# Loading the input in halves, warm-up matmuls and one-bank PSUM tiles in a GEGLU feed-forward kernel

## The chip, the cores and the metric

The kernel runs on one core of one Trainium2 chip. The metric is the device time of one execution in microseconds (us). The text gives the median of all executions of a kernel. A ratio is the mean time of one kernel's fast runs over the mean time of the kernel before's fast runs of the same rounds, so it is not quite the ratio of the medians quoted beside it. A profiled execution has a span 1.8 us shorter than its device time (309.2 against 310.99 us before), so spans are compared with spans.

PE is TensorE's matmul, PEld its weight load, DVE is VectorE, ACT is ScalarE, SPq is the sync engine's queue, which issues all transfers here. A transfer lands when all of its data has arrived. wg, wu and wd are the on-chip copies of w_gate, w_up and w_down.

## The reference

```python
B, S, D, F = 32, 32, 1024, 3584           # all bf16
def reference(x, w_gate, w_up, w_down):
    return (gelu_tanh(x @ w_gate) * (x @ w_up)) @ w_down
```

There are 1024 tokens. x is [1024, 1024] (2.1 MB), and each weight matrix has 3.67 million elements (7.3 MB).

## The kernel before

The kernel works in two phases. Phase one computes gate and up for one block of 128 features ("feature tile", ft, 28 of them) at a time, for all 1024 tokens, and forms gT, the product of the activated gate and up. Phase two multiplies gT by w_down. Weights come in chunks of 1, 3, 4, 4, 4, 4, 4, 4 feature tiles, with two buffers. A PSUM tile of 128x1024 f32 is two banks, and there are four such buffers.

```python
    for c in (1, 3):                       # first chunks; the rest are 4
        ...
    pspool = ctx.enter_context(tc.tile_pool(name="psum", bufs=4, space=PSUM))
    xT = xpool.tile([P, DT, N], bf16, name="xT")
    nc.sync.dma_start_transpose(out=xT[:, :, :], in_=xf)        # all of x at once
    ...
    for ci, FC in enumerate(chunks):
        nc.sync.dma_start(out=wg[:, :, :fw], in_=wg_r[:, :, f0 : f0 + fw])
        nc.sync.dma_start(out=wu[:, :, :fw], in_=wu_r[:, :, f0 : f0 + fw])
        for fl in range(FC):
            gate_ps = pspool.tile([P, N], fp32, name="gate_ps", tag="acc")   # two banks
            up_ps = pspool.tile([P, N], fp32, name="up_ps", tag="acc")
            for wt, ps in ((wg, gate_ps), (wu, up_ps)):
                for nb in range(NNB):              # two halves of 512 tokens
                    for dt in range(DT):           # 8 steps of 128 along D
                        nc.tensor.matmul(ps[:, nsl], lhsT=wt[:, dt, fsl],
                                         rhs=xT[:, dt, nsl], ...)
            # h, sq, w, z, s, hu, gT: three ACT and four DVE operations on [P, 1024]
            ...
        nc.sync.dma_start(out=wd[:, c0 : c0 + FC, :], in_=wd_r[:, c0 : c0 + FC, :])

    for tt in range(NT):
        out_ps = pspool.tile([P, D], fp32, name="out_ps", tag="acc")         # two banks
        for db in range(NDB):
            for ft in range(FT):
                nc.tensor.matmul(out_ps[:, dsl], lhsT=gT[:, ft, tsl], rhs=wd[:, ft, dsl], ...)
            o_sb = opool.tile([P, DB], bf16, name="o_sb", tag="o_sb")
            nc.vector.tensor_copy(o_sb, out_ps[:, dsl])
            nc.sync.dma_start(out=of[tsl, dsl], in_=o_sb)
```

## Time and profile before

| what | before |
|---|---|
| median time (the first 6 of 16 runs) | 310.92 us (310.54 to 312.26) |
| span of the profiled run | 309.2 us |
| PE busy | 291.7 us, 94% |
| first matmul starts | 12.02 us |
| last matmul ends, last copy starts | 305.92 us |

The first lines of the page give the span, and the busy time of each engine with its share of the span.

```profile
span 309.2 us, 3085 instructions
PE 291.7 (94%) x1318; PEld 131.9 (43%) x1344; DVE 95.9 (31%) x128; ACT 86.4 (28%) x86; POOL 0.2 (0%) x4
```

DVE and ACT are busy for a third of the time: PE is the bound. The chain that ended last shows where the rest of the span is. Its columns are start, length (us) and what ran.

```profile
0.73 7.53 SPq L80
8.32 3.65 DMA wg<-in_w_gate_dram
12.02 5.74 PE gate_ps L102 x16
17.75 3.45 PE up_ps L102 x16
...
251.87 10.74 PE out_ps L136 x49
262.66 10.82 PE out_ps L136 x49
...
298.93 0.70 DVE o_sb L144
299.68 6.22 PE out_ps L136 x28
305.92 0.69 DVE o_sb L144
```

Sixteen matmuls take 3.45 us, so one takes 0.216 us, and the 1344 matmuls of the kernel about 290.1 us. The first matmul waits 12.02 us, 7.53 of them for the queue to issue the x transpose. The first sixteen matmuls take 5.74 us, 2.29 more than sixteen later ones. At 298.93 PE waits for a copy of o_sb (0.78 us in the waits of PE). The copy, the store and the end of the kernel take 3.28 us after 305.92. One more detail was in plain sight and was passed over in the prediction: nearly all pieces of 49 matmuls in phase two take 10.82 us, but one takes 10.74.

The timeline of the weight loads shows why the first sixteen are slow. Its columns are start, length, engine, line, operation, count, and in brackets the idle time before it with what ended it.

```profile
12.42 0.15 PEld L102 LDWEIGHTS <-wg 128*128 128x128 bf16 x1 [0.28 <-issue]
...
15.83 0.15 PEld L102 LDWEIGHTS <-wg 128*128 128x128 bf16 x1 [0.28 <-issue]
16.26 1.00 PEld L102 LDWEIGHTS <-wg 128*128 128x128 bf16 x5 [0.28 <-issue]
```

From 12.03 to 16.26 us there are ten steps from one weight load to the next of about 0.427 us (the first is 0.39), twice the later 0.216 us (15.83 to 16.26 is the last such step). The Trainium skill, "TensorE: Matmul & The Clock Gate", Part 1, says that the PE starts at half clock and gets its full clock only after sustained activity of about 3.4 us. The trace agrees in kind: ten matmuls, 4.25 us, at half rate. The granted clock that the profile gives does not show it; it reads 1.00 in each of those microseconds.

### The profile page before, as it was taken

To read this page: it belongs to the slowest core of one execution; us is meant where nothing else is said; L and a number is where in the kernel's file an instruction comes from. 1 tells how busy PE (TensorE), PEld (TensorE's weight loads), DVE (VectorE), ACT (ScalarE), POOL (GpSimd) and SP (SyncE) were. 2 spreads that over 40 slices of the span, in tenths; PEclk is the share of its full clock that TensorE was granted. 3 is DMA by queue.
4 is the path that set the end of the run, shared out by engine and by line. 5 is a ranking of instruction groups with operands and counts; after the bars stand their busy time and mean duration, and the time that the engine had idled before them with its cause. 6 is when DMAs were issued, how large, how long until landed. Compare 5 with 4: busy or idle time off the path is not lost.

```text
span 309.2 us, 3085 instructions
## 1 busy us (share of the span) xinstructions
PE 291.7 (94%) x1318; PEld 131.9 (43%) x1344; DVE 95.9 (31%) x128; ACT 86.4 (28%) x86; POOL 0.2 (0%) x4
## 2 busy tenths in 40 slices
PE   0499999999999999999999999999999999999985
PEld 0144444444444444444444444444444444444442
DVE  0024333444443334444433334442001001100010
ACT  1045344444333444344334443440000000000000
POOL 0000000000000000000000000000000000000000
PEclk9999999999999999999999999999999999999999
DMA  8999994025006101700530000000000100000010
GB/s 197 258 354 371 389 325 144 2 84 188 0 2 209 64 2 27 244 0 2 157 114 2 0 0 0 2 0 17 19 17 17 34 19 17 17 34 19 17 34 17
DMA packets 30892, 26.40 MB, mean 85 GB/s; under 512 B 10912, under 2 KB 27296, under 8 KB 30880
## 3 DMA queue, kind: packets, MB, share of 16 engines
q1 hardware_dynamic: 30880, 26.22, 26.9%
q8 instruction: 10, 0.16, 0.2%
q14 instruction: 2, 0.02, 0.0%
HBM read 22.02 MB, written 2.10 MB: 78 GB/s over the span
## 4 chain that ended last, share of the span: by engine, by line
PE 94%; SPq 2%; DMA 1%; issue 1%; DVE 0%
PE gate_ps L102 32%; PE out_ps L136 31%; PE up_ps L102 31%; SPq L80 2%; DMA wg<-in_w_gate_dram 1%; DVE o_sb L144 0%
## 5 line engine op out<-in xcount | busy, mean ns | idle before, releaser
L102 PE MATMUL gate_ps<-xT,wg 128*128 128x512 bf16 x440 | 102.8, 385 | 12.4 <-DMA wg<-in_w_gate_dram 12.0
L102 PE MATMUL up_ps<-xT,wu 128*128 128x512 bf16 x439 | 100.6, 379 | 0.5
L136 PE MATMUL out_ps<-wd,gT 128*128 128x512 bf16 x439 | 97.1, 379 | 1.3 <-DVE o_sb L144 0.8
L102 PEld LDWEIGHTS <-wg 128*128 128x128 bf16 x448 | 44.3, 99 | 66.2 <-DMA wg<-in_w_gate_dram 12.0
L136 PEld LDWEIGHTS <-gT 128*128 128x128 bf16 x448 | 43.8, 98 | 54.4 <-issue 2.5
L102 PEld LDWEIGHTS <-wu 128*128 128x128 bf16 x448 | 43.8, 98 | 52.9
L111 ACT ACTIVATE h<-gate_ps 128x1024 bf16<-128x1024 f32 x28 | 28.7, 1024 | 84.9 <-PE gate_ps L102 82.3
L115 DVE TENSOR_SCALAR w<-sq 128x1024 bf16<-128x1024 bf16 x28 | 11.9, 426 | 111.7 <-ACT sq L113 111.7
L119 ACT ACTIVATE s<-z 128x1024 bf16<-128x1024 bf16 x28 | 29.6, 1057 | 36.5 <-DVE z L117 36.5
L144 DVE CAST o_sb<-out_ps 128x512 bf16<-128x512 f32 x16 | 11.1, 692 | 85.8 <-PE out_ps L136 85.8
L121 DVE TENSOR_TENSOR hu<-h,up_ps 128x1024 bf16<-128x1024 bf16 x28 | 34.2, 1221 | 8.4 <-PE up_ps L102 8.1
L113 ACT ACTIVATE sq<-gate_ps 128x1024 bf16<-128x1024 f32 x28 | 28.5, 1018 | 0.0
L122 DVE TENSOR_TENSOR gT<-hu,s 128x1024 bf16<-128x1024 bf16 x28 | 19.4, 692 | 3.9 <-ACT s L119 1.1
L117 DVE TENSOR_TENSOR z<-w,h 128x1024 bf16<-128x1024 bf16 x28 | 19.4, 692 | 0.9
L111 ACT ACT_TABLE_LOAD x1 | 1.3, 1283 | 0.7 <-PEq L160 0.7
L119 ACT ACT_TABLE_LOAD x1 | 1.3, 1283 | 0.0
L160 POOL MEMSET const-bfloat16-1.0<- 128x1 bf16 x1 | 0.1, 101 | 0.0
L160 POOL MEMSET const-uint8-127<- 128x1 uint8 x1 | 0.1, 101 | 0.0
L160 POOL MEMSET const-float32-0.0<- 128x1 f32 x1 | 0.1, 98 | 0.2 <-issue 0.2
L160 POOL MEMSET const-float32-1.0<- 128x1 f32 x1 | 0.1, 98 | 0.0
## 6 DMA issues: line engine op xcount, KB each, us to landing
wg<-in_w_gate_dram SPq DMA_DIRECT2D x6, 1024.0 KB, 5.3
wu<-in_w_up_dram SPq DMA_DIRECT2D x6, 1024.0 KB, 5.4
wd<-in_w_down_dram SPq DMA_DIRECT2D x6, 1024.0 KB, 11.9
out_dram<-o_sb SPq DMA_DIRECT2D x16, 128.0 KB, 1.7
wg<-in_w_gate_dram SPq DMA_DIRECT2D x1, 768.0 KB, 6.4
wu<-in_w_up_dram SPq DMA_DIRECT2D x1, 768.0 KB, 8.3
wd<-in_w_down_dram SPq DMA_DIRECT2D x1, 768.0 KB, 9.6
wg<-in_w_gate_dram SPq DMA_DIRECT2D x1, 256.0 KB, 3.7
```

What stands on the lines that cost most here:

```text
L80: nc.sync.dma_start_transpose(out=xT[:, :, :], in_=xf)
L102: nc.tensor.matmul(ps[:, nsl], lhsT=wt[:, dt, fsl], rhs=xT[:, dt, nsl], start=(dt == 0), stop=(dt == DT - 1),)
L111: nc.scalar.activation(h, gate_ps, ACT.Copy)
L113: nc.scalar.activation(sq, gate_ps, ACT.Square)
L115: nc.vector.tensor_scalar(w, sq, _C2A, _C2, ALU.mult, ALU.add)
L117: nc.vector.tensor_tensor(z, w, h, ALU.mult)
L119: nc.scalar.activation(s, z, ACT.Sigmoid)
L121: nc.vector.tensor_tensor(hu, h, up_ps, ALU.mult)
L122: nc.vector.tensor_tensor(gT[:, ft, :], hu, s, ALU.mult)
L136: nc.tensor.matmul(out_ps[:, dsl], lhsT=gT[:, ft, tsl], rhs=wd[:, ft, dsl], start=(ft == 0), stop=(ft == FT - 1),)
L144: nc.vector.tensor_copy(o_sb, out_ps[:, dsl])
L160: nc = _bacc.Bacc("TRN2", target_bir_lowering=False, num_devices=1)
```

## The change

The intent is to start PE earlier and with its clock up. The changed kernel
- transposes x in two halves of 512 tokens, and works through the first four feature tiles for the first half before it needs the second;
- runs 24 matmuls on a tile of zeros while the data arrives;
- uses first chunks of 2 and 2 feature tiles in place of 1 and 3;
- uses PSUM tiles of one bank (128x512) in 8 buffers for gate, up and out, and 3 work buffers in place of 2, so that each ACT and DVE operation of phase one handles half as many columns;
- loads wd in seven pieces of four feature tiles, from the third chunk on, and orders each but the last behind that chunk's weights, without a wait.

```diff
-    for c in (1, 3):
+    for c in (2, 2):
...
-    ework = ctx.enter_context(tc.tile_pool(name="ework", bufs=2))
+    ework = ctx.enter_context(tc.tile_pool(name="ework", bufs=3))
-    pspool = ... name="psum", bufs=4
+    pspool = ... name="psum", bufs=8
+    warm = xpool.tile([P, 512], bf16, name="warm")
+    nc.vector.memset(warm, 0.0)
+    warm_ps = pspool.tile([P, 512], fp32, name="warm_ps", tag="acc")
+    for _ in range(24):
+        nc.tensor.matmul(warm_ps, lhsT=warm[:, 0:P], rhs=warm, start=True, stop=True)
...
-    nc.sync.dma_start_transpose(out=xT[:, :, :], in_=xf)
+    def load_xT_block(nb):
+        nc.sync.dma_start_transpose(out=xT[:, :, nsl], in_=xf[nsl, :])
+    def load_wd(ft0, ft1, last_w):
+        ld = nc.sync.dma_start(out=wd[:, ft0:ft1, :], in_=wd_r[:, ft0:ft1, :])
+        tc.add_manual_dep(ld.ins, last_w.ins.name, <no-sync, data>, ...)
+    def mm1_and_eltwise(ft, nb):           # one feature tile, 512 tokens
+        gate_ps = pspool.tile([P, NB], fp32, name="gate_ps", tag="acc")
+        up_ps = pspool.tile([P, NB], fp32, name="up_ps", tag="acc")
+        ...                                # the same operations as before on [P, 512]
+    load_xT_block(0); load_w_chunk(0); load_w_chunk(1)
+    for ft in early_fts: mm1_and_eltwise(ft, 0)          # 4 feature tiles, first half
+    load_xT_block(1)
+    for ft in early_fts: mm1_and_eltwise(ft, 1)
+    for ci in range(2, NCH): load_w_chunk(ci); load_wd(...); both halves of each ft
...
-        out_ps = pspool.tile([P, D], fp32, name="out_ps", tag="acc")
         for db in range(NDB):
+            out_ps = pspool.tile([P, DB], fp32, name="out_ps", tag="acc")
```

(The loop lines are written shorter here than in the source; nothing else is left out that changes an instruction.)

More of the change, by code (lines that the diff above doesn't have):

```diff
@@ L63 @@
         acc += c
+    NCH = len(chunks)
     FC_MAX = max(chunks)
-    x_r = xf.rearrange("n (dt dp) -> n dt dp", dp=P)
     wg_r = w_gate.rearrange("(dt dp) f -> dp dt f", dp=P)
@@ L74, with load_w_chunk @@
     wpool = ctx.enter_context(tc.tile_pool(name="w", bufs=2))
-    ework = ctx.enter_context(tc.tile_pool(name="ework", bufs=2))
+    ework = ctx.enter_context(tc.tile_pool(name="ework", bufs=3))
     opool = ctx.enter_context(tc.tile_pool(name="osb", bufs=3))
-    pspool = ctx.enter_context(tc.tile_pool(name="psum", bufs=4, space=bass.MemoryType.PSUM))
+    pspool = ctx.enter_context(tc.tile_pool(name="psum", bufs=8, space=bass.MemoryType.PSUM))
+    warm = xpool.tile([P, 512], bf16, name="warm")
[3 more added lines that the diff above has]
+        nc.tensor.matmul(warm_ps, lhsT=warm[:, 0:P], rhs=warm, start=True, stop=True)
     xT = xpool.tile([P, DT, N], bf16, name="xT")
-    nc.sync.dma_start_transpose(out=xT[:, :, :], in_=xf)
     gT = gpool.tile([P, FT, N], bf16, name="gT")
     wd = wdpool.tile([P, FT, D], bf16, name="wd")
-    for ci, FC in enumerate(chunks):
+    def load_xT_block(nb):
+        nsl = slice(nb * NB, (nb + 1) * NB)
+        nc.sync.dma_start_transpose(out=xT[:, :, nsl], in_=xf[nsl, :])
+    w_tiles = {}
+    def load_w_chunk(ci):
         f0 = chunk_start[ci] * P
-        fw = FC * P
+        fw = chunks[ci] * P
         wg = wpool.tile([P, DT, FC_MAX * P], bf16, name="wg", tag="wg")
@@ L90 @@
         wu = wpool.tile([P, DT, FC_MAX * P], bf16, name="wu", tag="wu")
-        nc.sync.dma_start(out=wu[:, :, :fw], in_=wu_r[:, :, f0 : f0 + fw])
-        for fl in range(FC):
-            ft = chunk_start[ci] + fl
-            fsl = slice(fl * P, (fl + 1) * P)
-            gate_ps = pspool.tile([P, N], fp32, name="gate_ps", tag="acc")
-            up_ps = pspool.tile([P, N], fp32, name="up_ps", tag="acc")
-            for wt, ps in ((wg, gate_ps), (wu, up_ps)):
-                for nb in range(NNB):
-                    nsl = slice(nb * NB, (nb + 1) * NB)
-                    for dt in range(DT):
-                        nc.tensor.matmul(
-                            ps[:, nsl],
-                            lhsT=wt[:, dt, fsl],
-                            rhs=xT[:, dt, nsl],
-                            start=(dt == 0),
-                            stop=(dt == DT - 1),
-                        )
-            h = ework.tile([P, N], bf16, name="h", tag="h")
-            nc.scalar.activation(h, gate_ps, ACT.Copy)
-            sq = ework.tile([P, N], bf16, name="sq", tag="sq")
-            nc.scalar.activation(sq, gate_ps, ACT.Square)
-            w = ework.tile([P, N], bf16, name="w", tag="w")
-            nc.vector.tensor_scalar(w, sq, _C2A, _C2, ALU.mult, ALU.add)
-            z = ework.tile([P, N], bf16, name="z", tag="z")
-            nc.vector.tensor_tensor(z, w, h, ALU.mult)
-            s = ework.tile([P, N], bf16, name="s", tag="s")
-            nc.scalar.activation(s, z, ACT.Sigmoid)
-            hu = ework.tile([P, N], bf16, name="hu", tag="hu")
-            nc.vector.tensor_tensor(hu, h, up_ps, ALU.mult)
-            nc.vector.tensor_tensor(gT[:, ft, :], hu, s, ALU.mult)
@@ L124 @@
-        c0 = chunk_start[ci]
-        nc.sync.dma_start(
-            out=wd[:, c0 : c0 + FC, :],
-            in_=wd_r[:, c0 : c0 + FC, :],
-        )
+        last_w = nc.sync.dma_start(out=wu[:, :, :fw], in_=wu_r[:, :, f0 : f0 + fw])
+        w_tiles[ci] = (wg, wu)
+        return last_w
+    def load_wd(ft0, ft1, last_w):
+        ft1 = min(ft1, FT)
+        if ft0 >= ft1:
+            return
+        ld = nc.sync.dma_start(out=wd[:, ft0:ft1, :], in_=wd_r[:, ft0:ft1, :])
+        tc.add_manual_dep(
+            ld.ins,
+            last_w.ins.name,
+            mybir.DependencyInfo(mybir.DependencyClass.NoSync, mybir.DependencyReason.DATA),
+            reason="wd behind the weights of this chunk",
+        )
@@ new lines, in mm1_and_eltwise @@
+    def mm1_and_eltwise(ft, nb):
+        ci = max(i for i in range(NCH) if chunk_start[i] <= ft)
+        wg, wu = w_tiles[ci]
+        fl = ft - chunk_start[ci]
+        fsl = slice(fl * P, (fl + 1) * P)
+        nsl = slice(nb * NB, (nb + 1) * NB)
+        gate_ps = pspool.tile([P, NB], fp32, name="gate_ps", tag="acc")
+        up_ps = pspool.tile([P, NB], fp32, name="up_ps", tag="acc")
+        for wt, ps in ((wg, gate_ps), (wu, up_ps)):
+            for dt in range(DT):
+                nc.tensor.matmul(
+                    ps,
+                    lhsT=wt[:, dt, fsl],
+                    rhs=xT[:, dt, nsl],
+                    start=(dt == 0),
+                    stop=(dt == DT - 1),
+                )
+        h = ework.tile([P, NB], bf16, name="h", tag="h")
+        nc.scalar.activation(h, gate_ps, ACT.Copy)
+        sq = ework.tile([P, NB], bf16, name="sq", tag="sq")
+        nc.scalar.activation(sq, gate_ps, ACT.Square)
+        w = ework.tile([P, NB], bf16, name="w", tag="w")
+        nc.vector.tensor_scalar(w, sq, _C2A, _C2, ALU.mult, ALU.add)
+        z = ework.tile([P, NB], bf16, name="z", tag="z")
+        nc.vector.tensor_tensor(z, w, h, ALU.mult)
+        s = ework.tile([P, NB], bf16, name="s", tag="s")
+        nc.scalar.activation(s, z, ACT.Sigmoid)
+        hu = ework.tile([P, NB], bf16, name="hu", tag="hu")
+        nc.vector.tensor_tensor(hu, h, up_ps, ALU.mult)
+        nc.vector.tensor_tensor(gT[:, ft, nsl], hu, s, ALU.mult)
@@ new lines @@
+    load_xT_block(0)
+    load_w_chunk(0)
+    if NCH > 1:
+        load_w_chunk(1)
+    n_early = min(NCH, 2)
+    early_fts = list(range(chunk_start[0], chunk_start[n_early - 1] + chunks[n_early - 1]))
+    if NNB > 1:
+        for ft in early_fts:
+            mm1_and_eltwise(ft, 0)
+        for nb in range(1, NNB):
+            load_xT_block(nb)
+        wd_next = 0
+        for ft in early_fts:
+            for nb in range(1, NNB):
+                mm1_and_eltwise(ft, nb)
+    else:
+        wd_next = 0
+        for ft in early_fts:
+            mm1_and_eltwise(ft, 0)
@@ L130 @@
+    for ci in range(n_early, NCH):
+        last_w = load_w_chunk(ci)
+        load_wd(wd_next, wd_next + FC_MAX, last_w)
+        wd_next += FC_MAX
+        for fl in range(chunks[ci]):
+            ft = chunk_start[ci] + fl
+            for nb in range(NNB):
+                mm1_and_eltwise(ft, nb)
+    load_wd(wd_next, FT, last_w)
     for tt in range(NT):
         tsl = slice(tt * P, (tt + 1) * P)
-        out_ps = pspool.tile([P, D], fp32, name="out_ps", tag="acc")
         for db in range(NDB):
@@ L134 @@
             dsl = slice(db * DB, (db + 1) * DB)
+            out_ps = pspool.tile([P, DB], fp32, name="out_ps", tag="acc")
             for ft in range(FT):
                 nc.tensor.matmul(
-                    out_ps[:, dsl],
+                    out_ps,
                     lhsT=gT[:, ft, tsl],
@@ L143 @@
             o_sb = opool.tile([P, DB], bf16, name="o_sb", tag="o_sb")
-            nc.vector.tensor_copy(o_sb, out_ps[:, dsl])
+            nc.vector.tensor_copy(o_sb, out_ps)
             nc.sync.dma_start(out=of[tsl, dsl], in_=o_sb)
```

## The prediction

> **What bounds the kernel now.** The page's busy row: PE 291.7 of 309.2 us (94%); the chain of waits is 94% PE. 1344 matmuls of 128x512 run one every 0.216 us (chain: 16 in 3.45 us), so about 290.1 us is PE at its rate, and the change leaves these matmuls alone. The rest:
> - Start, 12.02 us: the chain shows 7.53 us of the sync queue issuing the x transpose, then 3.65 us until the first wg lands. In 1 us windows the transpose moves 290 GB/s from 2.15 us on; it lands at 10.3.
> - Cold clock: the first 16 matmuls take 5.74 us, later 16s 3.45: 2.3 us lost. In the timeline weight loads are 0.427 us apart for ten matmuls (12.0 to 16.3), then 0.216. The Trainium skill, "TensorE: Matmul & The Clock Gate", Part 1, has the PE at half clock until about 3.4 us of sustained activity; this trace agrees (4.3 us).
> - One PE wait of 0.78 us for the copy of o_sb before the last 28 matmuls.
> - About 0.8 us of small issue gaps.
> - Tail, 3.3 us: last matmul ends at 305.9, copy 0.69, store 1.7.
> No wait for weights or wd shows on PE after 12.02. ACT (86 us) and DVE (96 us) do not bound.
>
> **What the change does.**
> 1. x is transposed in halves; the first matmuls need one. Half of 2.1 MB at 290 GB/s is 3.6 us: moved by 5.8 us. But the first weight chunk doubles to 512 KB: 1.7 to 2.1 us at 250 to 300 GB/s, plus about 1 us to landing. Estimate: wg lands at 8.4 to 9.0, wu at 10 to 11.
> 2. 24 warm-up matmuls, from about 1.4 us. With the cold run seen here (10 x 0.427 + 14 x 0.216) they end at 8.7; 8.3 to 9.9 depending on when the clock rises. They add PE work in idle time and about meet the data: first real matmul at 9.0, already warm. Gain 3.0 + 2.3 us.
> 3. One-bank PSUM tiles: ACT and DVE operations double in count and halve in size; more fixed cost, off the critical path (under 2.7 us per 3.45 us half). Separate out_ps tiles remove the 0.78 us wait.
> 4. The second x half is due 13.8 us after the first matmul (22.8) and should land by 16 to 19. Chunk 2 loads once chunk 0 is done (19 to 20.7 us after the first matmul), is due at 27.6 and 29.3, and 1 MB takes 5.3 us: no stall. wd moves behind the weights; it was no PE wait before.
>
> **Critical path.** 12.02 to 9.0, minus 2.3, minus 0.8: 6.1 us, less 0.3 for possible short waits for wu: 5.8. Predicted 305.2 us (1.9% faster), 80% range 303.6 to 307.2. This is at the edge of 2%: faster by over 2% 0.30, within 2% 0.65, slower by over 2% 0.05.
>
> **What would show it.** First gate_ps matmul at about 9.0 us, 0.216 us spacing from the first; warm_ps matmuls from 1.4 to 8.7; under 1 us of PE idle afterwards; no o_sb wait; last matmul ending at about 300; tail still 3.3; half-size ACT and DVE operations over half of before's means.
>
> **What would make it wrong.** The second transpose held back until the matmuls on the first half are done (6 us stall at 22.8 and a cold restart: about 313 us); transpose or 512 KB loads landing later than scaled; a longer cold warm-up that holds up the real matmuls; PE gaps from a changed instruction order.

## The result, and the profile after

The changed kernel takes 305.02 us (median of 8 runs, 304.92 to 305.61), against 311.03 us for the kernel before over 16 runs. The ratio is 0.9802, 95% interval 0.9787 to 0.9817. That interval contains 0.98, so by the 2% rule it is neither clearly faster nor clearly within 2%; that it is faster at all is beyond doubt. The prediction of 305.2 us was right.

The same lines of the page after:

```profile
span 303.1 us, 3410 instructions
PE 295.9 (98%) x1341; PEld 134.0 (44%) x1368; DVE 108.9 (36%) x241; ACT 98.5 (32%) x170; POOL 0.2 (0%) x4
```

PE busy rose, because it now includes 7.0 us of warm-up; it is not a measure of progress here. DVE and ACT each do the same work in twice as many operations and are busy 12 to 13 us longer, at no cost. The chain after:

```profile
0.73 3.88 SPq L91
4.66 4.38 DMA wg<-in_w_gate_dram
9.09 1.90 PE gate_ps L127 x8
10.99 1.81 PE up_ps L127 x8
12.80 1.73 PE gate_ps L127 x8
...
284.59 10.74 PE out_ps L184 x49
295.38 4.06 PE out_ps L184 x18
299.46 0.69 DVE o_sb L192
```

The first gate matmul starts at 9.09 us, and eight matmuls take 1.90, 1.81 and then 1.73 us. The pieces of 49 take 10.74 us, and no copy interrupts them. The warm-up in the timeline of PE and PEld:

```profile
1.18 6.97 PE L83 MATMUL warm_ps<-warm 128*128 128x512 bf16 x24 [1.18 <-DVE warm L80]
4.14 0.15 PEld L83 LDWEIGHTS <-warm 128*128 128x128 bf16 x1 [0.28 <-issue]
4.53 3.12 PEld L83 LDWEIGHTS <-warm 128*128 128x128 bf16 x15 [0.24 <-issue]
9.09 1.90 PE L127 MATMUL gate_ps<-xT,wg 128*128 128x512 bf16 x8 [0.94 <-DMA wg<-in_w_gate_dram]
```

The slow stretch now lies in the warm-up, from 1.18 to 4.53 us. The warm-up ends at 8.15 us, and PE idles for only 0.94 us before the first wg lands. It began at 1.18 us and not at 1.4 as predicted, behind a short memset: the Trainium skill, "VectorE: DVE Perf Modes", Zero memsets can be issued as uint32 (trn2), says that zeros of a 2-byte type can be written as half as many uint32, and the trace agrees: the memset of the 128x512 bf16 warm tile is recorded as 128x256 uint32 and takes 272 ns.

The timeline of the weight loads in phase two answers why 10.82 became 10.74. First the kernel before:

```profile
275.35 11.96 PEld L136 LDWEIGHTS <-gT 128*128 128x128 bf16 x56 [0.20 <-issue]
287.51 11.10 PEld L136 LDWEIGHTS <-gT 128*128 128x128 bf16 x52 [0.20 <-issue]
299.68 5.71 PEld L136 LDWEIGHTS <-gT 128*128 128x128 bf16 x27 [1.06 <-issue]
```

And after, all of phase two in one line:

```profile
202.35 96.58 PEld L184 LDWEIGHTS <-gT 128*128 128x128 bf16 x448
```

Before, the stream of weight loads breaks once per output tile, seven times by 0.20 us and at last by 1.06 us. The compiled order of PE's instructions tells where (a count of its listing, by output tile and by waits):

```
kernel before, phase two, matmuls in a row:
28 tile 1, first half | 4 tile 2 | 28 tile 1, second half [waits DVE] | 24 tile 2 | 4 tile 3 | 28 tile 2, second half [waits DVE] | ...
... | 24 tile 8 | 28 tile 8, second half [waits DVE]
```

The second half of each two-bank tile waits until DVE has copied the first half, although they are different banks. For seven tiles the compiler put four matmuls of the next tile into the wait; for the last tile there was nothing to put there. The timeline from 214.15 to 214.6 us, at the first of the seven, shows that four matmuls were not quite enough:

```profile
213.77 0.69 DVE L144 CAST o_sb<-out_ps 128x512 bf16<-128x512 f32 x1 [4.03 <-PE out_ps L136]
...
214.22 0.10 PEld L136 LDWEIGHTS <-gT 128*128 128x128 bf16 x1
...
214.51 0.10 PEld L136 LDWEIGHTS <-gT 128*128 128x128 bf16 x1 [0.20 <-issue]
```

The copy starts when the first half is complete and ends at 214.46 us. The waiting matmul begins at 214.51, just behind it, although the four matmuls (0.86 us) would have let it begin at 214.43, one step of 0.216 after 214.22. The Trainium skill, "TensorE: Matmul & The Clock Gate", Part 2, says that PE pulls weight loads ahead of running matmuls, and the trace agrees: the load at 214.22 is the waiting matmul's own, made ahead of the wait, and the one at 214.51 belongs to the matmul after it (after the last break there are likewise 27 loads for 28 matmuls). So the break is the wait of the matmul itself, not a late load. The piece of 49 in which it falls takes 0.08 us longer (10.82 less 10.74). Seven of these are 0.56 us. Between two loads of the unbroken stream 0.12 us are idle (0.216 less 0.098 for a load), so the last break of 1.06 us costs 0.94. That is more than the 0.78 us in PE's waits, which count from the end of the matmul before, when the next one could already have been running.

The account of the 6.1 us between the spans, with the prediction beside it:

| term | predicted | traces |
|---|---|---|
| first real matmul, 12.02 to 9.09 us | 3.0 | 2.93 |
| slow first matmuls | 2.3 | 2.12 |
| copy before the last 28 matmuls | 0.8 | 0.94 |
| seven short waits in phase two | not seen | 0.56 |
| wait for the first wu | -0.3 | -0.08 |
| end of the kernel after the last matmul (3.28 to 3.64) | 0 | -0.36 |
| sum | 5.8 | 6.11 |

The -0.08 is 10.90 (first up matmul) less 9.09 + 8 x 0.216. In the profiles, from the start of the last copy to the end of the span took 3.3 to 3.6 us, and in runs 8 and 10 about 4.0 and 4.1, in kernels with the same end. What sets this was not found, so the -0.36 is no effect of the change that could be shown.

### The profile page after: what moved, and what is told of

Same layout as the page of the kernel before. It is cut to its first block, busy times and chain, and to the rows that moved or that the text cites. A ratio compares the mean times of both kernels' runs of the same rounds, so it can differ in the third digit from the quotient of the medians.

```text
span 303.1 us, 3410 instructions
## 1 busy us (share of the span) xinstructions
PE 295.9 (98%) x1341; PEld 134.0 (44%) x1368; DVE 108.9 (36%) x241; ACT 98.5 (32%) x170; POOL 0.2 (0%) x4
## 4 chain that ended last, share of the span: by engine, by line
PE 95%; DMA 1%; SPq 1%; issue 1%; DVE 0%
PE gate_ps L127 32%; PE up_ps L127 32%; PE out_ps L184 32%; DMA wg<-in_w_gate_dram 1%; SPq L91 1%; DVE o_sb L192 0%
## 5 line engine op out<-in xcount | busy, mean ns | idle before, releaser
L127 PE MATMUL up_ps<-xT,wu 128*128 128x512 bf16 x438 | 105.0, 379 | 0.5
L135 ACT ACTIVATE h<-gate_ps 128x512 bf16<-128x512 f32 x56 | 33.4, 597 | 55.3 <-PE gate_ps L127 53.6
L143 ACT ACTIVATE s<-z 128x512 bf16<-128x512 bf16 x56 | 35.3, 630 | 49.1 <-DVE z L141 49.1
L139 DVE TENSOR_SCALAR w<-sq 128x512 bf16<-128x512 bf16 x56 | 16.5, 295 | 82.5 <-ACT sq L137 82.5
L145 DVE TENSOR_TENSOR hu<-h,up_ps 128x512 bf16<-128x512 bf16 x56 | 38.0, 679 | 11.8 <-PE up_ps L127 11.8
L137 ACT ACTIVATE sq<-gate_ps 128x512 bf16<-128x512 f32 x56 | 33.1, 592 | 0.0
L146 DVE TENSOR_TENSOR gT<-hu,s 128x512 bf16<-128x512 bf16 x56 | 23.8, 425 | 9.3 <-ACT s L143 9.1
L141 DVE TENSOR_TENSOR z<-w,h 128x512 bf16<-128x512 bf16 x56 | 23.8, 425 | 1.9
L83 PE MATMUL warm_ps<-warm 128*128 128x512 bf16 x24 | 7.0, 460 | 1.2 <-DVE warm L80 1.2
L83 PEld LDWEIGHTS <-warm 128*128 128x128 bf16 x24 | 2.7, 114 | 5.0 <-issue 2.2
```

The costliest lines, as they stand in the source:

```text
L83: nc.tensor.matmul(warm_ps, lhsT=warm[:, 0:P], rhs=warm, start=True, stop=True)
L127: nc.tensor.matmul(ps, lhsT=wt[:, dt, fsl], rhs=xT[:, dt, nsl], start=(dt == 0), stop=(dt == DT - 1),)
L135: nc.scalar.activation(h, gate_ps, ACT.Copy)
L137: nc.scalar.activation(sq, gate_ps, ACT.Square)
L139: nc.vector.tensor_scalar(w, sq, _C2A, _C2, ALU.mult, ALU.add)
L141: nc.vector.tensor_tensor(z, w, h, ALU.mult)
```

## The experiments

Every run below gave the right result. Each call of several kernels had its own runs of the kernel before, with medians of 311.15, 311.42 and 311.45 us; the ratios are to those. The three calls ran on three chips, and the changed kernel was not run again in them. A difference from its 305.02 us is therefore one in which the kernel before moved by 0.4 us (311.03 to 311.45); where it is under 1 us, the traces have to bear it out.

### 1. No warm-up

```diff
-    warm = ...; nc.vector.memset(warm, 0.0); warm_ps = ...
-    for _ in range(24):
-        nc.tensor.matmul(warm_ps, lhsT=warm[:, 0:P], rhs=warm, start=True, stop=True)
```

> The changed kernel without the 24 warm-up matmuls, nothing else. My theory: the first wg still lands at about 9.1 us and the first real matmul still starts there, but the first ten or so real matmuls run at 0.427 us instead of 0.216, so the last matmul ends 1.7 to 2.5 us later and the time is about 307.3 us (305.0 + 2.3). Rival: the warm-up is only filler, and all of the gain is the earlier start and the PSUM tiles: 305.0 us.

Measured: 306.93 us, ratio 0.9864 (0.9847 to 0.9881), so 1.9 us more than the changed kernel. PE in the timeline:

```profile
8.95 3.59 PE L121 MATMUL gate_ps<-xT,wg 128*128 128x512 bf16 x8 [8.95 <-DMA wg<-in_w_gate_dram]
12.34 1.99 PE L121 MATMUL up_ps<-xT,wu 128*128 128x512 bf16 x8
```

The start is the same, and the first eight matmuls take 3.4 us to the next group's start where an eight at full rate takes 1.73. The warm-up is worth 1.9 us by itself; the rival falls.

### 2. x in one piece, and 3. the same with a longer warm-up

```diff
-    load_xT_block(0)
+    nc.sync.dma_start_transpose(out=xT[:, :, :], in_=xf)
...
-        for nb in range(1, NNB):
-            load_xT_block(nb)
```

The third kernel also has `range(44)` in place of `range(24)`.

> The changed kernel with x transposed in one piece at the start, warm-up of 24 kept. Theory: the first wg lands at about 12.9 us (9.1 + 3.8, half of x at 290 GB/s), and as the warm-up ends at about 8.2 us, PE is idle for 4.7 us and its clock falls back, so the first ten real matmuls are slow again: 305.0 + 3.8 + 2.3 = 311.1 us, so the warm-up is worth nothing here. Rival A: the clock stays up over the gap: 308.8 us. Rival B: the halves of x are worth nothing because the doubled first weight chunk eats them: 305 to 306 us.

> As the run with x in one piece, but with 44 warm-up matmuls, which end at about 8.2 + 20 x 0.216 = 12.5 us and so reach the data at about 12.9. Theory: start at about 12.9 us and warm: 308.8 us, 2.3 less than with 24 warm-up matmuls. Rival (the clock does not fall back in a gap of 4.7 us): the same as with 24.

Measured: 310.18 us with 24 warm-up matmuls, ratio 0.9971 (0.9954 to 0.9989), and 308.73 us with 44, ratio 0.992 (0.9903 to 0.9937). PE with 24:

```profile
1.18 7.05 PE L83 MATMUL warm_ps<-warm 128*128 128x512 bf16 x24 [1.18 <-DVE warm L80]
12.74 3.59 PE L127 MATMUL gate_ps<-xT,wg 128*128 128x512 bf16 x8 [4.51 <-DMA wg<-in_w_gate_dram]
16.13 2.97 PE L127 MATMUL up_ps<-xT,wu 128*128 128x512 bf16 x8
```

And with 44:

```profile
1.18 12.28 PE L83 MATMUL warm_ps<-warm 128*128 128x512 bf16 x44 [1.18 <-DVE warm L80]
13.29 1.89 PE L127 MATMUL gate_ps<-xT,wg 128*128 128x512 bf16 x7
```

With 24 the clock rose during the warm-up, PE then idled for 4.51 us, and the first real matmuls were slow again. Here the profile shows the clock itself: the granted clock, in windows of 1 us, is 1.00 up to 11 us, 0.74 from 11 to 12, 0.50 from 12 to 18, 0.85 from 18 to 19 and then 1.00. The slow real matmuls lie in that stretch. One of these windows (start and end, length, then busy us and instructions of PE, PEld, DVE, ACT and POOL, then the granted clock, the share of DMA and GB/s):

```profile
14.00:15.00 1.00, 1.00 (x4) 0.44 (x3) 0.00 (x0) 0.00 (x0) 0.00 (x0) 0.50 1.16 291
```

With 44 the first real matmuls were fast. So a warm-up has to reach the data. The Trainium skill (the same page, Part 1) puts the idle time that costs the clock at about 3.4 us; here 4.51 us cost it, and 0.94 us in the changed kernel (1.70 us in run 9) did not. Comparing run 3 with the changed kernel, where both are warm, the halves of x are worth 3.7 us. In the profile of run 3 the long warm-up held the first real matmul to 13.29 us, about 0.5 us after the first wg had landed (12.80), and the end of the kernel was 0.3 us shorter, so the cleaner figure is the start: 12.74 us in run 2 against 9.09, 3.65 us, close to the 3.8 expected for half of x at 290 GB/s.

The six runs of run 2 split: two at 311.1 us with a mean granted clock of 0.988, four at 310.0 to 310.3 with 0.992 to 0.994. This suggests that the length of the second slow stretch varies from run to run; the miss against 311.1 would then be the shorter stretches. The profile shown is one of the two long ones.

### 4. Kernel before, one-bank out_ps only

```diff
-        out_ps = pspool.tile([P, D], fp32, name="out_ps", tag="acc")
         for db in range(NDB):
             dsl = slice(db * DB, (db + 1) * DB)
+            out_ps = pspool.tile([P, DB], fp32, name="out_ps", tag="acc")
```

> The kernel before with one-bank out_ps tiles of 128x512 and nothing else. Theory: the 0.78 us wait of PE for the copy of o_sb before the last 28 matmuls goes, as no matmul writes a tile that the copy still reads, and the time falls by 0.8 us to about 310.2 us; the order of the instructions on PE is no longer interleaved between two output tiles. Rival: the wait is one for the copy engine or the store and comes back elsewhere: 311.0 us.

Measured: 309.95 us against 311.15, ratio 0.9956 (0.9939 to 0.9973), which is 1.4 us. The chain in phase two:

```profile
284.41 10.74 PE out_ps L136 x49
...
295.20 9.67 PE out_ps L136 x44
...
304.90 0.69 DVE o_sb L144
```

The wait before the last 28 matmuls is gone, and so are the seven short ones: all pieces of 49 take 10.74 us. The expectation of 0.8 us missed the second part; 0.94 + 0.56 = 1.50 us fits the measured 1.4, although the interval of the ratio (0.8 to 1.9 us) would not tell the two apart by itself. The trace does.

### 5. Kernel before, 42 warm-up matmuls only

```diff
+    warm = xpool.tile([P, 512], bf16, name="warm")
+    nc.vector.memset(warm, 0.0)
+    warm_ps = pspool.tile([P, 512], fp32, name="warm_ps", tag="acc")
+    for _ in range(42):
+        nc.tensor.matmul(warm_ps, lhsT=warm[:, 0:P], rhs=warm, start=True, stop=True)
```

> The kernel before with 42 warm-up matmuls (about 1.2 to 12.1 us) and nothing else. Theory: the first real matmul still starts at about 12.1 us, but warm, so the first 16 take 3.45 us and the time falls by about 2.3 us to 308.8 us. Rival: the slow first matmuls come from the data still arriving (x and weights moving into the same memory), not from the clock: 311 us and 16 in 5.7 us as before.

Measured: 309.68 us against 311.42, ratio 0.9949 (0.9929 to 0.9969), so 1.7 us less. PE:

```profile
1.18 12.15 PE L83 MATMUL warm_ps<-warm 128*128 128x512 bf16 x42 [1.18 <-DVE warm L80]
13.16 3.62 PE L108 MATMUL gate_ps<-xT,wg 128*128 128x512 bf16 x15
```

The first real matmuls are fast while the same data is still arriving as before, so the rival falls: it was the clock. The slow matmuls cost 2.12 us in the trace before, not 2.3, and at least in this execution the warm-up itself took back 1.1: 14 of its matmuls were slow, not 10, so that it ended after the data had landed (first wg at 8.55 + 3.6 = 12.15 us) and held up the first real matmul to 13.16 us, against 12.02. It is one of three executions at 309.9 to 310.1 us; the other three, at 309.1 to 309.5, were not profiled. A fixed number of warm-up matmuls is a bet on when the clock rises.

### 6. No ordering of wd

```diff
-        tc.add_manual_dep(ld.ins, last_w.ins.name, <no-sync, data>, reason="wd behind the weights of this chunk")
```

> The changed kernel without the added ordering of wd behind the weights. The compiled order then puts five wd loads (5 MB) ahead of the third chunk's wg and wu on the sync queue. Theory: wd fills DMA time between 17 and 32 us that was empty (DMA moved nothing from 18 to 28 us), wg of the third chunk lands at about 35 us, before it is due at 36.7, so the time stays at 305.0 us and the ordering is worth nothing here. Rival: the third chunk's weights come late behind wd and PE waits 1 us or more: over 306 us.

Measured: 305.83 us, ratio 0.9824 (0.98 to 0.9847), 0.8 us more than the changed kernel. Of PE's waits, one is new:

```profile
PE up_ps L121 <- DMA wu<-in_w_up_dram: 1.1, 1, 1.1
```

Five wd loads went first, wg of the third chunk came in time to within 0.1 us (its matmuls begin at 36.60), and wu landed 9.76 us after its issue, at 39.55, when PE could have used it at 38.33 (36.60 + 8 x 0.216). The expectation was wrong for wu: the ordering is worth about 1 us, not nothing (the last copy starts at 300.54 us, against 299.46 in the changed kernel). In the kernel before, the compiled order had put five early wd loads behind the third chunk's weights by itself, and PE had no such wait.

### 7. Fewer buffers

```diff
-    ework bufs=3, psum bufs=8
+    ework bufs=2, psum bufs=4
```

> The changed kernel with 4 one-bank PSUM buffers in place of 8 and 2 work buffers in place of 3. Theory: a half takes PE 3.45 us and its copies out of PSUM are done within about 2.7 us of its last matmul, so two halves in flight are enough and the time stays at 305.0 us: the added buffers are no part of the gain. Rival: with half as much PSUM PE waits for ACT or DVE in every half, 0.2 us or more each over 56 halves: over 310 us.

Measured: 305.22 us, ratio 0.9805 (0.9784 to 0.9827), the changed kernel's 0.9802 within its interval. The waits of PE are the same two kinds as in the changed kernel, for the warm tile and the first wg. The larger number of buffers is no part of the gain. The smaller out_ps tiles are one (run 4). Smaller gate and up tiles were not run alone; after the first sixteen matmuls the weight loads of phase one before show no break that they could remove.

### 8. A still earlier start

```diff
-    load_xT_block(0)
-    load_w_chunk(0)
+    load_ft(wg0, wg_r, 0)                  # 256 KB
+    for dh in range(2):                    # first 512 tokens, by halves of D
+        nc.sync.dma_start_transpose(out=xT[:, dh*4:(dh+1)*4, 0:NB], in_=xf[0:NB, dh*512:(dh+1)*512])
+    load_ft(wu0, wu_r, 0)
+    load_ft(wg0, wg_r, 1); load_ft(wu0, wu_r, 1)
...
-    for _ in range(24):
+    for _ in range(14):
```

> A further step: the first feature tile's wg (256 KB) is loaded first, then the first half of x in two pieces of 512 rows by 512 features, then the first wu and the rest of chunk 0 by single feature tiles; 14 warm-up matmuls. Theory: what still delays the first matmuls is the transfer of 1 MB of x and 512 KB of weights ahead of them. Now the first four matmuls can start at about 5.6 to 6 us, the next four at about 7.5, and the first gate tile is done at about 8.4 instead of 10.8 us, so that the time falls by about 2.4 us to 302.6 us. Rival: smaller pieces land so much later (the 256-byte rows and the smaller transposes) that the start gains under 1 us: 304 us or more.

Measured: 304.35 us, ratio 0.978 (0.9759 to 0.9802). That is 0.7 us less than the changed kernel, not 2.4: neither theory's number, nearer to the rival's. PE:

```profile
7.01 1.03 PE L127 MATMUL gate_ps<-xT,wg 128*128 128x512 bf16 x4
8.30 1.02 PE L127 MATMUL gate_ps<-xT,wg 128*128 128x512 bf16 x4 [0.26 <-DMA xT<-in_x_dram]
9.85 1.90 PE L127 MATMUL up_ps<-xT,wu 128*128 128x512 bf16 x8 [0.52 <-DMA wu<-in_w_up_dram]
11.58 1.89 PE L127 MATMUL gate_ps<-xT,wg 128*128 128x512 bf16 x8
```

The second piece of x lands just before 8.30 us instead of 7.5, and wu before 9.85 instead of about 8.4. (All 14 warm-up matmuls were slow here and held the first real one to 7.01 us, about 0.7 after the first piece of x had landed; as PE then waits for the second piece, this costs nothing.) In windows of 1 us the transfers moved only 161 GB/s from 5 to 6 us and 194 from 7 to 8, around the changes from one transfer to the next, where 290 was assumed throughout. What in the transfer causes these dips was not tested. By the second feature tile PE is 1.06 us ahead of the changed kernel (11.58 against 12.64 us), and it is still 1.05 us ahead when the last copy starts (298.41 against 299.46). The end of the kernel after that took 3.99 us in this profile, against 3.64, which leaves the 0.7 us that the spans show (302.4 against 303.1).

### 9. First chunks of 1 and 3 again

```diff
-    for c in (2, 2):
+    for c in (1, 3):
...
-    for _ in range(24):
+    for _ in range(18):
```

> The changed kernel with the old first chunks (1 and 3 feature tiles in place of 2 and 2) and 18 warm-up matmuls, so that a long slow run of the warm-up still ends by about 7.9 us. Theory: the first wg is 256 KB instead of 512 KB and lands about 0.8 us earlier, at about 8.2 us, the first wu at about 9.1; the first real matmul starts at 8.2 and the time falls to about 304.3 us. Rival: the landing of the first wg is fixed by the transpose ahead of it and not by its size: 305.0 us.

Measured: 305.96 us, ratio 0.9827 (0.9806 to 0.9848): about 0.9 us slower than the changed kernel, where 0.7 faster was expected. PE:

```profile
8.56 1.90 PE L127 MATMUL gate_ps<-xT,wg 128*128 128x512 bf16 x8 [1.70 <-DMA wg<-in_w_gate_dram]
12.97 1.90 PE L127 MATMUL gate_ps<-xT,wg 128*128 128x512 bf16 x8 [0.79 <-DMA wg<-in_w_gate_dram]
15.25 1.68 PE L127 MATMUL up_ps<-xT,wu 128*128 128x512 bf16 x7 [0.38 <-DMA wu<-in_w_up_dram]
```

The first wg did land earlier, by 0.5 us. But with one half of x, a chunk of one feature tile feeds PE for 3.45 us only, and the second chunk's 768 KB pieces land too late: two waits of PE, 1.17 us, and 1.5 us of late starts (12.97 instead of 12.01, and 15.25 instead of 14.70). The last copy starts at 300.36 us, 0.90 later than in the changed kernel. The intervals of the two ratios overlap a little; the traces do not leave it open. I had costed the first landing and not the second. The chunks of 2 and 2 belong to the halves of x.

### 10. and 11. Another order of the early loads, and a smaller last block

```diff
     load_ft(wg0, wg_r, 0)
+    load_ft(wu0, wu_r, 0)                  # moved ahead of x
     ... two pieces of x
-    load_ft(wu0, wu_r, 0)
-    for _ in range(14):
+    for _ in range(12):
```

Run 11 in addition:

```diff
+        # last tt: output blocks of 512, 256 and 256 columns instead of 512 and 512
```

> As the earlier-start run, but the first wg and the first wu (256 KB each) both go ahead of the two quarter pieces of x, so that the queue switches between plain loads and transposes once less before the first gate tile, and 12 warm-up matmuls. Theory: the second piece of x lands at about 8.5 us, gate ends at 9.4 and up, which no longer waits for wu, at 11.1 (11.6 in the earlier-start run), so 303.9 us. Rival: wu in front only moves the wait to x, and the first two tiles end no sooner: 304.3 us or more.

> The same with the last output block of 128x512 made as two of 128x256, so that after the last matmul only a half-size copy and a half-size store remain. Theory: the copy takes about 0.4 us in place of 0.69 and the store a little less, so 0.3 us less than without: about 303.6 us. Rival: the 56 matmuls of 256 columns run slower than 28 of 512, as the weight loads no longer hide behind them, and the gain is lost: 303.9 us or more.

Measured: 304.26 us for run 10, ratio 0.9786 (0.976 to 0.9811), and 303.54 us for run 11, ratio 0.9755 (0.9733 to 0.9777). Run 10 does not differ from run 8 in time: the wait moved from wu to x, as the rival had it (PE waits 1.06 us for x). In the trace the next feature tile does begin sooner, at 11.25 us instead of 11.58, and the last copy too (298.08 against 298.41); the time of the whole does not show it. Run 11 is the fastest kernel, and its interval lies wholly below 0.98. The copy at the end is what was expected, here the timeline of DVE in run 11:

```profile
295.29 0.42 DVE L215 CAST o_sb<-out_ps 128x256 bf16<-128x256 f32 x1 [2.36 <-PE out_ps L207]
298.35 0.43 DVE L215 CAST o_sb<-out_ps 128x256 bf16<-128x256 f32 x1 [2.63 <-PE out_ps L207]
```

The two copies are 3.06 us apart, so the 56 small matmuls cost PE almost nothing (2 x 3.06 against 6.04 between the copies of full blocks), and the last copy is 0.26 us shorter than the 0.69 of a full block. The medians of the two runs differ by 0.7 us. The shorter copy explains 0.3 of it. The rest is in the end of the kernel behind the last copy, which was long in the profile of run 10 (4.12 us from the start of the copy) and not in that of run 11 (3.45 us); its cause stays open, and the intervals of the two ratios overlap. So the split of the last block by itself is not shown to be worth more than 0.3 us.

## Why the prediction was right

- **PE bounds the kernel and the change leaves its 1344 matmuls alone.** Right. The rate of 0.216 us per matmul is the same after, and the gain came from the edges of PE's work alone.
- **The halves of x and the first weight chunk bring the first matmul to about 9.0 us.** Right: 9.09. Alone, with PE warm in both, the halves of x are worth about 3.7 us (run 3 against the changed kernel; 3.65 by the starts). Run 9 shows that the doubled first chunk, which I had counted only as a cost of this step, earns more than it costs.
- **The warm-up removes 2.3 us and about meets the data.** Right in mechanism and nearly in size: 2.12 in the traces (2.3 counted the end of a last matmul with it). Runs 1 and 5 put it at 1.9 and 1.7 us, and run 2 shows the clock at 0.50 while matmuls are slow. Runs 2 and 3 show that it must reach the data, run 5 that it must not overrun it. The slow stretch was 8 matmuls in the profiled run of the changed kernel and 14 in that of run 5, so 24 is a sensible middle and no more.
- **Separate out_ps tiles remove 0.78 us.** Right mechanism, too small: the last wait costs 0.94, and they also remove seven short waits, 0.56 us together (run 4 and the two traces). This is the one term of the sum that was missed, though 10.82 beside 10.74 in the chain before would have shown it.
- **0.3 us of waiting for wu.** It was 0.08. The gain that was missed (0.56, 0.14 and 0.22 us) and the gain that did not come (0.18 of the slow matmuls, 0.07 of the start, 0.36 of the tail) nearly cancelled. That the total of 5.8 us was closer (6.0 between the medians) than its parts is luck.
- **Smaller tiles and more operations cost nothing, more buffers are not the point.** Right: h takes 597 ns instead of 1024 for half the columns, hu 679 instead of 1221, and PE never waits for them; run 7.
- **The second half of x and the third chunk arrive in time.** Right as built: the second transpose landed at 8.91 + 9.0 = 17.9 us, due at about 22.9. I had taken the ordering of wd to be without effect on PE; run 6 shows that without it PE waits 1.1 us for wu.
- **Near the edge of 2%.** The ratio of 0.9802 is on it.

## What to carry to other kernels

When one engine is busy 94% of the time at its own rate, the gain left is at its edges: cut what the first instruction must wait for, let filler work raise the clock during that wait and end just as the data lands, and keep the last instruction's copy and store small. A smaller first transfer helps only as long as the next one still arrives before the work on the first is done, so cost the second and third landing too. Give each independent block its own tile, so that no copy of one block holds up the work on the next, and look for small regular losses in a chain of equal pieces (10.82 beside 10.74): they add up.

## What the Trainium skill lacked or had wrong

- "TensorE: Matmul & The Clock Gate", Part 1, describes the transition as around 4 us into activity, within 0.5 us from run to run. Here the slow stretch in the profiled runs was 3.35 us (8 matmuls, changed kernel) to about 5.9 us (14 matmuls, run 5). Its remark that the number of slow matmuls varies by run, with 6, 11 and 14, fits better.
- The same page, Part 2, has weight loads pulled ahead of running matmuls, but does not say by how many. Here it was one load and no more whenever a matmul waited: in run 10 the first real load is at 5.85 us, and the second at 7.54, with the first real matmul, though its weights had landed long before.
- "DMA: Bandwidth & Descriptors", Latency and other measured facts, gives 261 GB/s for a transposing transfer with a non-contiguous middle dimension and 350 to 400 otherwise. Here a transposing load of x ran at 290 GB/s in the middle, and the page does not have the dips at the change from a transpose to plain loads (164 GB/s in the microsecond from 6 to 7 us of the changed kernel, between 287 and 316). Which of the page's two cases this load is was not tested.
